# Chunked attention into a token mixer on one core: one more period of stagger between exp and its transposes, and the last batch first in the drain

## The chip, the cores and the metric

One core of a Trainium2 chip runs the whole program. The metric is device time in microseconds. The engines are named as in the profile: PE (TensorE matmuls), PEld (its weight loads), DVE (VectorE), ACT (ScalarE), POOL (GpSimd, which here issues the loads), SP (which issues the stores).

## The reference, cut to what matters

```python
# q, k, v: (8, 8, 576, 64) = batch, heads, tokens, head_dim
# attention inside chunks of 64 tokens: 9 chunks a head
scores = matmul(q_c, k_c.T) / 8
attn   = exp(scores - max(scores)); attn = attn / (sum(attn) + 1e-9)
x      = matmul(attn, v_c)                # then heads side by side: (8, 576, 512)
# token mixer, batch by batch
wq, wk = x @ w_q, x @ w_k                 # (576, 64) each
mixed  = (wq @ wk.T / 8) @ x              # no softmax: the kernel forms wk.T @ x first
out    = relu(mixed) @ w_out              # (8, 576, 512) float32
```

## The kernel before, in words

**Attention.** The 576 chunks (8 batches, 8 heads, 9 chunks) are done 16 at a time in 36 units `u`, 4.5 units to a batch. A unit goes through these stages, each a function of its own:

- `stage_a1`: 16 transposes on PE of q and k into `tp`; `stage_a2`: DVE copies `tp` to `qkt`.
- `stage_b1`: 16 matmuls of 64x64 for the scores into `sp`, DVE takes the row maxima `mx`; `stage_b2`: DVE subtracts them (`sh`), ACT takes exp (`es`).
- `stage_c`: 4 transposes of `es` on PE into `ep`, ACT copies them to `et`.
- `stage_d1`: 16 matmuls with v into `xp` (a column of ones in v gives the row sums); `stage_d2`: three DVE steps (`den`, `rec`, `x_nat`) divide and write the result to the resident `x_nat`.

`tp`, `sp`, `ep` and `xp` have one PSUM buffer each; three more, the tag `m`, serve all steps of the mixer.

**Mixer.** For each batch `make_moe(b)` makes small steps, here called by short names: `xt0`, `xt1`, `xt2` (`p_xt`: six transposes of `x_nat`, one ACT copy of 128x768), `wqk0`, `wqk1` (`p_wqk`: the two projections in two halves; after the second, ACT copies `wqkT` in two pieces and DVE copies `wqd` from it), `wkn` (`p_wkn`: transposes of wk, a DVE copy), `g` (`p_g`: wk.T @ x, an ACT copy), `mix0`, `mix1`, `mixt` (`p_mixed`, `p_mixed_tail`: the mixing matmuls and their relus on ACT), `out0` to `out3` and `outT` (`p_out`, `p_out_tail`: the output projection, an ACT copy `osb`, a store from SP). A full `out` is four matmuls of 512 columns; before, it is cut in two halves.

**Order.** The schedule is manual: every engine runs its instructions in the order in which the Python code emits them. The loop over `kk` makes one period of each unit's stages, and `fill(kk, place, budget)` puts mixer steps between them. The dictionary `plan` gives a step its period and place; the outputs of finished batches wait in `outs` and are taken while a budget lasts. In one period before, PE sees: b1(kk), d1(kk-1), place 0, a1(kk+2), places 1 and 2, c(kk), place 3. DVE sees mx(kk), sh(kk), the three steps of d2(kk-1), the copy of a2(kk+2); ACT sees exp(kk) ahead of the copies of places 1 and 2, then et(kk). After the last period a drain loop emits what is left, in plan order, with outputs between the steps of the chain by estimated costs and due times.

**Loads.** POOL issues the loads of batches 0 to 5 at the start, those of batches 6 and 7 from inside the loop, when the buffers of batches 0 and 1 have been read. The last pieces of batch b are first needed by `stage_a1` of the unit that holds its first chunks, two periods ahead of that unit's b1.

In a cycle of nine periods (two batches) PE's mixer work before is, by the plan, with half outputs written a and b and the position of c marked:

```
16: 2.wkn | 3.xt0 1.out0b c 1.out1a      21: 3.g 4.xt0 2.out1b c 2.out2a
17: 2.g 1.out1b 1.out2a c 1.out2b        22: 3.mix0 | 4.xt1 2.out2b c 2.out3a
18: 2.mix0 | 3.xt1 1.out3a c 1.out3b     23: 3.mix1 | 3.mixt 2.out3b c
19: 2.mix1 | 2.mixt 3.xt2 c 3.wqk0 wqk1  24: 2.outT 4.xt2 3.out0a c 4.wqk0 wqk1
20: 3.wkn | 1.outT 2.out0a 2.out0b c 2.out1a
```

(Left of the bar: place 0, ahead of a1.)

Of the kernel before, what the change touches and what calls it, by code (L numbers as in the profile page):

```python
# [10 lines left out]
F32 = mybir.dt.float32  # L11
AF = mybir.ActivationFunctionType
ALU = mybir.AluOpType
# [4 lines left out]
def kernel(  # L18
# [15 lines left out]
    nc = tc.nc  # L34
# [89 lines left out]
    for b in range(2, 6):  # L124
        loads.append(load(b, None))

    def make_moe(b):
        st = {}

# [18 lines left out]
        def p_wqk(half):  # L148
            def run():
                xt = st["xt"]  # L150
                if half == 0:
                    st["pa"] = m_psum.tile([P, 512], F32, name="wpa", tag="m")
                    st["pb"] = m_psum.tile([P, CH], F32, name="wpb", tag="m")
                pa, pb = st["pa"], st["pb"]
                for i in (2 * half, 2 * half + 1):
                    flags = dict(start=(i == 0), stop=(i == HQ - 1))
                    nc.tensor.matmul(
                        pa[:, :], lhsT=wqk16[:, i, :], rhs=xt[:, NC_ * i : NC_ * i + 8, :], **flags
                    )
                    nc.tensor.matmul(  # L160
                        pb[:, :], lhsT=wqk16[:, i, :], rhs=xt[:, NC_ * i + 8, :], **flags
                    )
                if half == 0:
                    return
                wqkT = moe_pool.tile([P, S], F16, name="wqkT", tag="wqkT")
                wqd = moe_pool.tile([P, S], F16, name="wqd", tag="wqd")
                nc.scalar.copy(wqkT[:, 0:512], pa[:])
                nc.scalar.copy(wqkT[:, 512:S], pb[:])  # L168

                nc.vector.tensor_copy(wqd[CH:P, :], wqkT[0:CH, :])  # L170
                st["wqkT"], st["wqd"] = wqkT, wqd

            return run
# [36 lines left out]
        def p_mixed(w):  # L210
            def run():
                if w == 0:
                    st["rmx"] = moe_pool.tile([P, HQ, S], F16, name="rmx", tag="rmx")
                g16, rmx = st["g16"], st["rmx"]
                wq = (st["wqkT"][0:CH], st["wqd"][CH:P])
                ms = []
                for par in range(2):
                    ma = m_psum.tile([P, 512], F32, name=f"ma{par}", tag="m")
                    nc.tensor.matmul(  # L219
                        ma[:], lhsT=g16[CH * par : CH * par + CH, w, :], rhs=wq[par][:, 0:512]  # L220
                    )
                    ms.append(ma)
                for par in range(2):
                    nc.scalar.activation(  # L224

                        rmx[:, 2 * w + par, 0:512].rearrange("p (c g r) -> p c g r", g=G, r=R),
                        ms[par][:].rearrange("p (c r g) -> p c g r", g=G, r=R),
                        AF.Relu,
                        scale=scale_moe,
                    )  # L230

            return run

        def p_mixed_tail():
            g16, rmx = st["g16"], st["rmx"]
            wq = (st["wqkT"][0:CH], st["wqd"][CH:P])
            for par in range(2):
                mb = m_psum.tile([P, 2, CH], F32, name=f"mb{par}", tag="m")
                for w in range(2):
                    nc.tensor.matmul(  # L240
                        mb[:, w], lhsT=g16[CH * par : CH * par + CH, w, :], rhs=wq[par][:, 512:S]
                    )
                nc.scalar.activation(
                    rmx[:].rearrange("p (w two) s -> p w two s", two=2)[
                        :, :, par, 512:S
                    ].rearrange("p w (g r) -> p w g r", g=G, r=R),
                    mb[:].rearrange("p w (r g) -> p w g r", g=G, r=R),
                    AF.Relu,
                    scale=scale_moe,
                )  # L250

        def p_out(t, half):
            def run():
                rmx = st["rmx"]
                if half == 0:
                    st["op"] = m_psum.tile([P, DM], F32, name="op", tag="m")
                op = st["op"]
                for i in (2 * half, 2 * half + 1):
                    nc.tensor.matmul(  # L259
                        op[:],  # L260
                        lhsT=rmx[:, i, ds(t * P, P)],
                        rhs=wout16[:, i, :],
                        start=(i == 0),
                        stop=(i == HQ - 1),
                    )
                if half == 0:
                    return
                osb = osb_pool.tile([P, DM], F32, name="osb", tag="osb")
                nc.scalar.copy(osb[:], op[:])  # L269
                nc.sync.dma_start(out[b, ds(t * P, P), :], osb[:])  # L270

            return run

        def p_out_tail():
# [21 lines left out]


        chain = [
            (1, 2, 0.4, 0.4, xts[2]),
            (1, 3, 0.5, 0.2, p_wqk(0)),  # L300
            (1, 3, 0.5, 0.6, p_wqk(1)),
            (2, 0, 0.4, 1.2, p_wkn),
            (3, 1, 0.7, 0.9, p_g),
            (4, 0, 0.25, 0.8, p_mixed(0)),
            (5, 0, 0.25, 1.2, p_mixed(1)),
            (5, 1, 0.15, 0.2, p_mixed_tail),
        ]
        outs = [(2, 0.45, p_out(t, half)) for t in range(4) for half in range(2)]
        outs.append((1, 0.5, p_out_tail))
        return xts[:2], chain, outs  # L310

# [73 lines left out]
    def stage_d1(u):  # L385
        et = state[u]["et"]
        xp = x_psum.tile([P, 2, 512], F32, name="xp", tag="xp")
        xv = xp[:, :, 0 : 4 * 65].rearrange("p l (m e) -> p l m e", e=65)
        for m in range(4):
            b, s = divmod(4 * u + m, NS)  # L390
            vt = data[b][1]
            for sl in range(2):
                for par in range(2):
                    rows = slice(CH * par, CH * par + CH)
                    nc.tensor.matmul(  # L395
                        xv[rows, sl, m, :],
                        lhsT=et[rows, m, CH * sl : CH * sl + CH],
                        rhs=vt[rows, sl, s, 0 : D + 1],
                        start=True,
                        stop=True,  # L400
                    )
        state[u]["xv"] = xv
# [17 lines left out]


    moes = [make_moe(b) for b in range(B)]
    ends = [-(-NS * (b + 1) // 4) for b in range(B)]
    plan = {}
    for b in range(B):
        for g in range(2):
            plan.setdefault((-(-(NS * b + 6 * (g + 1)) // 4) + 1, 2), []).append(
                (b, 0.4, 0.0, moes[b][0][g])
            )
        for n, (at, place, cost, wait, step) in enumerate(moes[b][1]):  # L430
            plan.setdefault((ends[b] + at, place), []).append((b, cost, wait, step))
    opened = [0] * B
    outs = []

    def run(entry):
        b, cost, _, step = entry
        step()
        opened[b] += 1
        if opened[b] == 2 + len(moes[b][1]):
            outs.extend(moes[b][2])  # L440
        return cost

    def fill(kk, place, budget):
        spent = sum(run(x) for x in plan.pop((kk, place), []))
        while outs and outs[0][0] == min(place, 2) and spent < budget:
            _, cost, step = outs.pop(0)
            step()
            spent += cost

    for u in range(2):  # L450
        stage_a1(u)
        stage_a2(u)
    for kk in range(NU + 1):
        if kk < NU:
            stage_b1(kk)
        if kk >= 1:
            stage_d1(kk - 1)
        fill(kk, 0, 0.0)
        if kk + 2 < NU:
            stage_a1(kk + 2)  # L460
        if kk < NU:
            stage_b2(kk)
        if kk >= 1:
            stage_d2(kk - 1)
        if kk + 2 < NU:
            stage_a2(kk + 2)
        fill(kk, 1, 0.1)
        fill(kk, 2, 0.8)
        if kk < NU:
            stage_c(kk)  # L470
        fill(kk, 3, 0.4)
        for b in range(B - 6):
            if ends[b] == kk:
                data[b + 6] = load(b + 6, None)

    chain = [x for key in sorted(plan) for x in plan[key]]
    clock, due = 0.0, 0.0
    while chain or outs:
        if chain and (not outs or clock >= due + chain[0][2]):
            entry = chain.pop(0)  # L480
            clock = due = max(clock, due) + run(entry)
        else:
            _, cost, step = outs.pop(0)
            step()
            clock += cost
# [28 lines left out]
```

## Time and profile before

| | |
|---|---|
| median of 3 runs | 187.09 us (185.51 to 187.12) |
| the profiled execution | 186.61 us; span of its instructions 184.8 us |
| busy over the span | PE 79%, DVE 61%, ACT 57%, PEld 50%, POOL 30% |

A row of the timeline has: start in us from the start of the span, duration in us, engine, line, operation, what it writes and reads, how many instructions were merged into the row, and in brackets the idle time of the engine before it with what ended it. PE's matmuls are pipelined, so the distance from one step's start to the next one's start, and not the duration, is what a step takes of PE. The waits list names the waiting instruction, what it waited for, the total in us, how often, and the longest.

### The profile page before, as it was taken

How to read it: one execution, taken by the hardware profiler on the slowest of the kernel's cores; microseconds unless marked ns; L12 is line 12 of the kernel's file. 1: busy time of each engine (PE TensorE's matmuls, PEld its weight loads, DVE VectorE, ACT ScalarE, POOL GpSimd, SP SyncE). 2: the span in 40 equal slices, each digit the busy share in tenths (PEclk: the TensorE clock that was granted, in tenths of full speed). 3: DMA queues.
4: the chain of work that ended last, by engine and by line, in shares of the span. 5: the costliest groups of instructions: out<-in, count | busy, mean ns of one | idle time of the engine just before them, and what ended most of it. 6: DMA issues, size and time to landing. Idle time of an engine off the chain costs nothing. (4 is left out here: it accounts for less than half of the span.)

```text
span 184.8 us, 5746 instructions
## 1 busy us (share of the span) xinstructions
PE 145.2 (79%) x2496; PEld 92.7 (50%) x2496; DVE 112.0 (61%) x233; ACT 105.2 (57%) x209; POOL 55.1 (30%) x68
## 2 busy tenths in 40 slices
PE   0355897896879897969899869798998695988781
PEld 0242675675645555636556546464554463434330
DVE  0123887767984878687868685877686757321000
ACT  2001334454584696647946876479468764584661
POOL 8999999733452603523000000000000000000000
PEclk9999999999999999999999999999999999699999
DMA  3999999999999999999999912032021120232515
GB/s 28 100 123 141 114 144 164 189 181 164 183 163 182 170 233 214 190 190 205 223 210 173 195 59 86 32 122 80 3 89 57 60 88 11 103 131 90 179 71 188
DMA packets 82041, 24.62 MB, mean 133 GB/s; under 512 B 76384, under 2 KB 77920, under 8 KB 82016
## 3 DMA queue, kind: packets, MB, share of 16 engines
q0 software_dynamic: 76128, 14.81, 95.5%
q1 hardware_dynamic: 5888, 9.44, 14.9%
q8 instruction: 19, 0.31, 0.6%
q14 instruction: 6, 0.05, 0.1%
HBM read 29.62 MB, written 9.44 MB: 211 GB/s over the span
## 5 line engine op out<-in xcount | busy, mean ns | idle before, releaser
L373 ACT ACTIVATE es<-sh 128x512 f16<-128x512 f32 x36 | 22.7, 630 | 48.6 <-DVE sh L365 24.3
L327 PE MATMUL tp<-ident,qn 128*64 128x128 f16 x576 | 29.9, 245 | 12.1 <-DMA qn<-in_q_dram 8.4
L259 PE MATMUL op<-wout,rmx 128*128 128x512 f16 x128 | 36.4, 388 | 1.3 <-ACT rmx L224 0.8
L359 DVE TENSOR_REDUCE mx<-sp 128x8 f32<-128x512 f32 x36 | 24.9, 692 | 15.6 <-PE sp L351 15.3
L337 DVE COPY qkt<-tp 128x1024 f16<-128x1024 f16 x36 | 24.5, 682 | 15.7 <-PE tp L327 15.7
L327 PEld LDWEIGHTS <-qn 128*64 128x64 f16 x576 | 21.2, 122 | 18.5 <-DMA qn<-in_q_dram 9.4
L365 DVE TENSOR_TENSOR sh<-sp,mx 128x512 f32<-128x512 f32 x36 | 24.9, 690 | 2.3 <-DVE mx L359 0.5
L410 DVE TENSOR_TENSOR x_nat<-xp,rec 128x512 f16<-128x512 f32 x36 | 24.9, 691 | 1.2
L382 ACT COPY et<-ep 128x512 f16<-128x512 f16 x36 | 21.5, 596 | 6.8 <-PE ep L380 6.4
L380 PE MATMUL ep<-ident,es 128*128 128x128 f16 x144 | 16.0, 241 | 10.0 <-ACT es L373 9.9
L395 PE MATMUL xp<-vt,et 64*64 64x65 f16 x576 | 16.9, 202 | 7.9 <-ACT et L382 7.5
L269 ACT COPY osb<-op 128x512 f32<-128x512 f32 x32 | 19.0, 592 | 5.1 <-PE op L259 2.6
L224 ACT ACTIVATE rmx<-ma 128x512 f16<-128x512 f32 x32 | 17.3, 596 | 8.1 <-PE ma L219 8.1
L380 PEld LDWEIGHTS <-es 128*128 128x128 f16 x144 | 10.4, 107 | 20.5 <-ACT es L373 18.2
L144 ACT COPY xt<-tx 128x768 f16<-128x768 f16 x23 | 18.4, 798 | 2.6 <-PE tx L137 2.5
L395 PEld LDWEIGHTS <-et 64*64 64x64 f16 x576 | 13.0, 115 | 11.4 <-ACT et L382 10.7
L351 PEld LDWEIGHTS <-qkt 64*64 64x64 f16 x576 | 13.0, 116 | 10.4 <-issue 9.2
L351 PE MATMUL sp<-qkt 64*64 64x64 f16 x576 | 17.2, 204 | 0.0
L95 POOL DMA_DIRECT2D vt<-in_v_dram x6 | 11.0, 1835 | 12.7 <-issue 8.0
L259 PEld LDWEIGHTS <-rmx 128*128 128x128 f16 x128 | 10.6, 99 | 7.4 <-issue 2.7
L137 PE MATMUL tx<-ident,x_nat 128*128 128x128 f16 x144 | 13.1, 231 | 1.0 <-ACT rmx L224 0.8
L170 DVE COPY wqd<-wqkT 64x576 f16<-64x576 f16 x8 | 2.8, 354 | 16.3 <-ACT wqkT L168 16.3
(49 smaller groups left out, 163.5 us busy)
## 6 DMA issues: line engine op xcount, KB each, us to landing
out_dram<-osb SPq DMA_DIRECT2D x32, 256.0 KB, 2.2
qn<-in_q_dram POOLq DMA_DIRECT2D x6, 576.0 KB, 18.2
qn<-in_k_dram POOLq DMA_DIRECT2D x6, 576.0 KB, 18.8
vt<-in_v_dram POOLq DMA_DIRECT2D x6, 576.0 KB, 19.5
out_dram<-osbt SPq DMA_DIRECT2D x16, 64.0 KB, 2.1
wout<-in_moe_w_out_dram POOLq DMA_DIRECT2D x2, 256.0 KB, 7.8
qn<-in_q_dram POOLq DMA_DIRECT2D x4, 96.0 KB, 3.2
qn<-in_k_dram POOLq DMA_DIRECT2D x4, 96.0 KB, 3.5
```

The lines of the kernel that those rows point to most:

```text
L259: nc.tensor.matmul(op[:], lhsT=rmx[:, i, ds(t * P, P)], rhs=wout16[:, i, :], start=(i == 0), stop=(i == HQ - 1),)
L269: nc.scalar.copy(osb[:], op[:])
L327: nc.tensor.transpose(tp[CH * sl : CH * sl + CH, j, ti, :, r, :], src[:, sl, t, r * D : r * D + D], ident[:],)
L337: nc.vector.tensor_copy(qkt[:].rearrange("p j t c k -> p (j t c k)"), tp[:].rearrange("p j t c r g -> p (j t c r g)"),)
L351: nc.tensor.matmul(sp[rows, i, :], lhsT=qkt[rows, j, 0, c, :], rhs=qkt[rows, j, 1, c, :], start=True, stop=True,)
L359: nc.vector.tensor_reduce(mx[:], sp[:], axis=AX.X, op=ALU.max)
L365: nc.vector.tensor_tensor(out=sh[:].rearrange("p i (g r) -> p i r g", g=G, r=R), in0=sp[:].rearrange("p i (r g) -> p i r g", g=G, r=R), in ...
L373: nc.scalar.activation(es[:], sh[:], AF.Exp, scale=scale_attn)
L380: nc.tensor.transpose(ep[:, m, :], es[:, 2 * m : 2 * m + 2, :], ident[:])
L382: nc.scalar.copy(et[:], ep[:])
L395: nc.tensor.matmul(xv[rows, sl, m, :], lhsT=et[rows, m, CH * sl : CH * sl + CH], rhs=vt[rows, sl, s, 0 : D + 1], start=True, stop=True,)
L410: nc.vector.tensor_tensor(out=x_nat[:, 4 * u : 4 * u + 4, :, :].rearrange("p m l d -> p l m d"), in0=xv[:, :, :, 0:D], in1=rec[:, :, :, No ...
```

## The change

Unit kk's transposes of exp, `stage_c`, move from the end of period kk to the middle of period kk+1, ahead of `stage_b2`; `stage_d1` and `stage_d2` follow one period later, and the loop has one period more. The places inside a period are ordered anew, the outputs are no longer halved and are taken only if they fit the budget, and the plan's dates are recomputed by `period`. In the last batch (`b == B - 1`) half of the relus, the small `wqkT` copy and every second `osb` copy go to DVE. The drain now runs the last batch's steps as soon as their due time comes, with everything else as filling.

```diff
+    def relu(on_vector, to, of):
+        if on_vector:
+            nc.vector.tensor_scalar(to, of, scale_moe, 0.0, op0=ALU.mult, op1=ALU.max)
+        else:
+            nc.scalar.activation(to, of, AF.Relu, scale=scale_moe)
...
-                nc.scalar.copy(wqkT[:, 512:S], pb[:])
+                (nc.vector.tensor_copy if b == B - 1 else nc.scalar.copy)(wqkT[:, 512:S], pb[:])
...
-                    nc.scalar.activation(
+                    relu(
+                        b == B - 1 and par == 1,
...
-        def p_out(t, half):
+        def p_out(t):
...
-                for i in (2 * half, 2 * half + 1):
+                for i in range(HQ):
...
-                nc.scalar.copy(osb[:], op[:])
+                (nc.vector.tensor_copy if b == B - 1 and t % 2 else nc.scalar.copy)(osb[:], op[:])
...
         chain = [
-            (1, 2, 0.4, 0.4, xts[2]),
-            (1, 3, 0.5, 0.2, p_wqk(0)),
-            (1, 3, 0.5, 0.6, p_wqk(1)),
+            (1, 2, 0.4, 0.2, xts[2]),
+            (1, 2, 0.5, 0.4, p_wqk(0)),
+            (1, 2, 0.5, 0.0, p_wqk(1)),
             (2, 0, 0.4, 1.2, p_wkn),
             (3, 1, 0.7, 0.9, p_g),
             (4, 0, 0.25, 0.8, p_mixed(0)),
-            (5, 0, 0.25, 1.2, p_mixed(1)),
-            (5, 1, 0.15, 0.2, p_mixed_tail),
+            (5, 0, 0.25, 0.8, p_mixed(1)),
+            (5, 1, 0.15, 0.5, p_mixed_tail),
         ]
-        outs = [(2, 0.45, p_out(t, half)) for t in range(4) for half in range(2)]
+        outs = [(2, 0.9, p_out(t)) for t in range(4)]
...
-    ends = [-(-NS * (b + 1) // 4) for b in range(B)]
+        period = lambda slots: -(-slots // 4) + 1
...
-        while outs and outs[0][0] == min(place, 2) and spent < budget:
+        while outs and outs[0][0] == place and spent + outs[0][1] <= budget:
...
-    for kk in range(NU + 1):
+    for kk in range(NU + 2):
         if kk < NU:
             stage_b1(kk)
-        if kk >= 1:
-            stage_d1(kk - 1)
+        if kk >= 2:
+            stage_d1(kk - 2)
         fill(kk, 0, 0.0)
         if kk + 2 < NU:
             stage_a1(kk + 2)
+        fill(kk, 1, 0.7)
+        if 1 <= kk <= NU:
+            stage_c(kk - 1)
         if kk < NU:
             stage_b2(kk)
-        if kk >= 1:
-            stage_d2(kk - 1)
+        if kk >= 2:
+            stage_d2(kk - 2)
         if kk + 2 < NU:
             stage_a2(kk + 2)
-        fill(kk, 1, 0.1)
-        fill(kk, 2, 0.8)
-        if kk < NU:
-            stage_c(kk)
-        fill(kk, 3, 0.4)
+        fill(kk, 2, 1.4 if len(outs) < 4 else 1.9)
...
-    chain = [x for key in sorted(plan) for x in plan[key]]
+    rest = [x for key in sorted(plan) for x in plan[key]]
+    last = [x for x in rest if x[0] == B - 1]
+    rest = [x for x in rest if x[0] < B - 1]
     clock, due = 0.0, 0.0
-    while chain or outs:
-        if chain and (not outs or clock >= due + chain[0][2]):
-            entry = chain.pop(0)
+    while last or rest or outs:
+        if last and (clock >= due + last[0][2] or not (rest or outs)):
+            entry = last.pop(0)
             clock = due = max(clock, due) + run(entry)
+        elif rest:
+            clock += run(rest.pop(0))
```

By the new plan PE's mixer work in nine periods is as follows; the first bar stands for a1, and c(kk-1) stands where it is written:

```
16: | c 2.xt2 2.wqk0 2.wqk1              21: 3.wkn | c 2.out0 2.out1
17: 2.wkn | c 3.xt0 1.out2               22: | 3.g c 4.xt0 2.out2
18: | 2.g c 1.out3                       23: 3.mix0 | c 4.xt1 2.out3
19: 2.mix0 | 1.outT c 3.xt1              24: 3.mix1 | 3.mixt 2.outT c 3.out0 3.out1
20: 2.mix1 | 2.mixt c 3.xt2 3.wqk0 wqk1
```

In the last periods and the drain it is:

```
35: b1 d1(33) 6.wkn c(34) 7.xt0 5.out2
36: d1(34) 6.g c(35) 5.out3
37: d1(35) 6.mix0 5.outT 7.xt1
drain: 6.mix1 7.xt2 6.mixt 6.out0 7.wqk0 7.wqk1 6.out1 6.out2 7.wkn 6.out3 7.g 6.outT
       7.mix0 7.mix1 7.mixt 7.out0 7.out1 7.out2 7.out3 7.outT
```

More of the change, by code (lines that the diff above doesn't have):

```diff
@@ L223, in run @@
                 for par in range(2):
-                    nc.scalar.activation(
+                    relu(
+                        b == B - 1 and par == 1,
                         rmx[:, 2 * w + par, 0:512].rearrange("p (c g r) -> p c g r", g=G, r=R),
                         ms[par][:].rearrange("p (c r g) -> p c g r", g=G, r=R),
-                        AF.Relu,
-                        scale=scale_moe,
                     )
@@ L242, in p_mixed_tail @@
                     )
-                nc.scalar.activation(
+                relu(
+                    b == B - 1 and par == 1,
                     rmx[:].rearrange("p (w two) s -> p w two s", two=2)[
@@ L247, in p_mixed_tail @@
                     mb[:].rearrange("p w (r g) -> p w g r", g=G, r=R),
-                    AF.Relu,
-                    scale=scale_moe,
                 )
-        def p_out(t, half):
+        def p_out(t):
             def run():
                 rmx = st["rmx"]
-                if half == 0:
-                    st["op"] = m_psum.tile([P, DM], F32, name="op", tag="m")
-                op = st["op"]
-                for i in (2 * half, 2 * half + 1):
+                op = m_psum.tile([P, DM], F32, name="op", tag="m")
+                for i in range(HQ):
                     nc.tensor.matmul(
@@ L265, in run @@
                     )
-                if half == 0:
-                    return
                 osb = osb_pool.tile([P, DM], F32, name="osb", tag="osb")
-                nc.scalar.copy(osb[:], op[:])
+                (nc.vector.tensor_copy if b == B - 1 and t % 2 else nc.scalar.copy)(osb[:], op[:])
                 nc.sync.dma_start(out[b, ds(t * P, P), :], osb[:])
@@ L422 @@
     moes = [make_moe(b) for b in range(B)]
-    ends = [-(-NS * (b + 1) // 4) for b in range(B)]
     plan = {}
     for b in range(B):
+        period = lambda slots: -(-slots // 4) + 1
         for g in range(2):
-            plan.setdefault((-(-(NS * b + 6 * (g + 1)) // 4) + 1, 2), []).append(
+            plan.setdefault((period(NS * b + 6 * (g + 1)) + 1, 2), []).append(
                 (b, 0.4, 0.0, moes[b][0][g])
             )
-        for n, (at, place, cost, wait, step) in enumerate(moes[b][1]):
-            plan.setdefault((ends[b] + at, place), []).append((b, cost, wait, step))
+        for at, place, cost, wait, step in moes[b][1]:
+            plan.setdefault((period(NS * (b + 1)) + at, place), []).append((b, cost, wait, step))
     opened = [0] * B
@@ L460 @@
             stage_a1(kk + 2)
+        fill(kk, 1, 0.7)
+        if 1 <= kk <= NU:
+            stage_c(kk - 1)
         if kk < NU:
             stage_b2(kk)
-        if kk >= 1:
-            stage_d2(kk - 1)
+        if kk >= 2:
+            stage_d2(kk - 2)
         if kk + 2 < NU:
             stage_a2(kk + 2)
-        fill(kk, 1, 0.1)
-        fill(kk, 2, 0.8)
-        if kk < NU:
-            stage_c(kk)
-        fill(kk, 3, 0.4)
+        fill(kk, 2, 1.4 if len(outs) < 4 else 1.9)
         for b in range(B - 6):
-            if ends[b] == kk:
+            if 4 * (kk - 1) >= NS * (b + 1) > 4 * (kk - 2):
                 data[b + 6] = load(b + 6, None)
-    chain = [x for key in sorted(plan) for x in plan[key]]
+    rest = [x for key in sorted(plan) for x in plan[key]]
+    last = [x for x in rest if x[0] == B - 1]
+    rest = [x for x in rest if x[0] < B - 1]
     clock, due = 0.0, 0.0
-    while chain or outs:
-        if chain and (not outs or clock >= due + chain[0][2]):
-            entry = chain.pop(0)
+    while last or rest or outs:
+        if last and (clock >= due + last[0][2] or not (rest or outs)):
+            entry = last.pop(0)
             clock = due = max(clock, due) + run(entry)
+        elif rest:
+            clock += run(rest.pop(0))
         else:
```

## The prediction

> **What bounds the kernel now.** I read the page's totals first, then the waits, then one cycle of nine periods in the windows view and in PE's timeline.
>
> ```profile
> PE 145.2 (79%) x2496; PEld 92.7 (50%) x2496; DVE 112.0 (61%) x233; ACT 105.2 (57%) x209; POOL 55.1 (30%) x68
> ```
> ```profile
> 76.75:114.19 37.44, 32.40 (x627) 20.72 (x625) 28.09 (x58) 25.59 (x52) 4.22 (x3) 1.00 1.48 171
> ```
> ```profile
> PEld L380 <- ACT es L373: 18.2, 25, 1.9
> DVE wqd L170 <- ACT wqkT L168: 16.3, 8, 3.4
> PEld L395 <- ACT et L382: 10.7, 21, 0.8
> ```
>
> The second row is the cycle from b1(16) to b1(25): 37.44 us, of which PE is busy 32.40, DVE 28.09, ACT 25.59. PE is nearest to full, but idle for 5 us, and the waits say on what: stage c's weight loads wait for exp (18.2 us in the run), stage d1's for et (10.7). Both come from doing exp, c, et and d1 within little more than a period. The middle row is another kind: DVE stops in front of `wqd` until ACT has copied `wqkT`, about 2 us in each batch, and the next period's mx stands behind it. What PE needs without waits is read from starts in its timeline:
>
> ```profile
> 76.75 0.44 PE L351 MATMUL sp<-qkt 64*64 64x64 f16 x16
> ...
> 77.46 0.40 PE L184 MATMUL wknp<-ident,wqkT 64*128 64x64 f16 x8
> ...
> 77.94 0.64 PE L327 MATMUL tp<-ident,qn 128*64 128x128 f16 x16
> ...
> 80.73 0.40 PE L380 MATMUL ep<-ident,es 128*128 128x128 f16 x4 [1.28 <-ACT es L373]
> ...
> 83.23 0.60 PE L199 MATMUL gp<-x_nat,wkn 128*64 128x256 f16 x8
> ...
> 83.99 1.04 PE L259 MATMUL op<-wout,rmx 128*128 128x512 f16 x4
> 84.86 0.39 PE L380 MATMUL ep<-ident,es 128*128 128x128 f16 x4
> 85.09 0.59 PE L259 MATMUL op<-wout,rmx 128*128 128x512 f16 x2
> 85.61 0.44 PE L351 MATMUL sp<-qkt 64*64 64x64 f16 x16
> 85.98 0.44 PE L395 MATMUL xp<-vt,et 64*64 64x65 f16 x16
> 86.35 0.39 PE L219 MATMUL ma<-wqkT,g 64*128 64x512 f16 x1
> ...
> 86.67 0.64 PE L327 MATMUL tp<-ident,qn 128*64 128x128 f16 x16
> 87.24 0.51 PE L137 MATMUL tx<-ident,x_nat 128*128 128x128 f16 x6
> 87.59 0.59 PE L259 MATMUL op<-wout,rmx 128*128 128x512 f16 x2
> ...
> 95.33 0.60 PE L281 MATMUL opt<-wout,rmx 128*64 128x256 f16 x8
> 95.86 1.04 PE L259 MATMUL op<-wout,rmx 128*128 128x512 f16 x4
> ...
> 112.94 0.38 PE L157 MATMUL wpa<-xt,wqk 128*128 128x512 f16 x1
> ...
> 114.19 0.44 PE L351 MATMUL sp<-qkt 64*64 64x64 f16 x16
> ```
>
> From each start to the next: b1 0.37, d1 0.37, mix 0.32, a1 0.57, xt 0.35, wkn 0.48, g 0.76, out 0.87, c 0.23, outT 0.53, both halves of wqk 1.25. `mixt` has no undisturbed row; I put it at 0.40, between c's 0.23 and wkn's 0.48. The row at 80.73 shows the wait to be removed: 1.28 us in front of c(16).
>
> **The steady part after the change.** In the new order c(kk-1) needs the exp of the period before, and d1 the et of the period before. Exp stands ahead of the copies of place 2 on ACT, so both are ready when PE comes: I cost these two waits at nothing, covered by a whole period of PE work. PE's base is b1 + d1 + a1 + c = 1.54; with the plan's steps the nine periods 16 to 24 sum to
>
> 16: 3.14, 17: 3.24, 18: 3.17, 19: 2.74, 20: 3.86, 21: 3.76, 22: 3.52, 23: 3.08, 24: 4.53; together 31.0.
>
> That is a floor. Two other things are late next.
>
> ```profile
> 46.10 0.69 DVE L359 TENSOR_REDUCE mx<-sp 128x8 f32<-128x512 f32 x1
> ...
> 49.11 0.69 DVE L359 TENSOR_REDUCE mx<-sp 128x8 f32<-128x512 f32 x1
> ```
> ```profile
> L189 DVE COPY wkn<-wknp 128x576 f16<-128x576 f16 x2 | 0.9, 448 | 0.0
> ```
> ```profile
> 115.00 0.30 DVE L170 COPY wqd<-wqkT 64x576 f16<-64x576 f16 x1 [1.84 <-ACT wqkT L168]
> ...
> 115.33 0.69 DVE L359 TENSOR_REDUCE mx<-sp 128x8 f32<-128x512 f32 x1
> ```
>
> DVE, back to back, takes 3.01 us from one mx to the next (46.10 to 49.11), and 3.45 with wkn's copy. And `wqd` stays where it was, at the end of its period: wqk ended at 114.19, the next mx began 1.14 us later, at 115.33. Ahead of that the second half of wqk now waits for xt2's copy, which on ACT stands behind et and exp:
>
> ```profile
> L373 ACT ACTIVATE es<-sh 128x512 f16<-128x512 f32 x36 | 22.7, 630 | 48.6 <-DVE sh L365 24.3
> L382 ACT COPY et<-ep 128x512 f16<-128x512 f16 x36 | 21.5, 596 | 6.8 <-PE ep L380 6.4
> L269 ACT COPY osb<-op 128x512 f32<-128x512 f32 x32 | 19.0, 592 | 5.1 <-PE op L259 2.6
> L224 ACT ACTIVATE rmx<-ma 128x512 f16<-128x512 f32 x32 | 17.3, 596 | 8.1 <-PE ma L219 8.1
> L144 ACT COPY xt<-tx 128x768 f16<-128x768 f16 x23 | 18.4, 798 | 2.6 <-PE tx L137 2.5
> ```
>
> Period 16, from b1: sh ends at about 1.9 (b1's 0.44, then mx and sh at 0.7 each), exp at 2.55, xt2's copy at 3.35, the second half of wqk at 4.0, the next mx 1.14 later; less the half microsecond by which an undisturbed mx trails its b1, 4.65 from mx to mx. In period 20 ACT also has two relus of `mix1` and the small ones of `mixt` ahead of et: the copy ends near 4.4 and PE near 5.0, but DVE comes out of periods 17 to 19 already late, so I take 5.1 from mx to mx, bounded by 4.65 and by 5.7, the sum without that lateness. The periods then become, each the larger of PE's and DVE's: 4.65, 3.45, 3.17, 3.01, 5.1, 3.76, 3.52, 3.08, 4.53, sum 34.3. Changing from out to b1 costs PE some 0.09 more (85.09 to 85.61 is 0.52 for two matmuls where four took 0.87), five times: 34.7 against 37.44.
>
> From period 8 (mx at 46.10) to b1(35) at 155.75, whose mx comes half a microsecond later, there are three such nines, the first with fewer outputs: 110.1 us now, 3 x 34.7 = 104.1 after. **Steady part: -6.0 us.** Ends: -7.3 without the 0.09s, about 0 if the waits come back elsewhere.
>
> **The start gains nothing.** Up to period 7 loads set the pace:
>
> ```profile
> 30.28 1.35 POOL L91 DMA_DIRECT2D qn<-in_k_dram  x1
> ```
> ```profile
> DMA to landing us min/median/max: 10.4/18.8/20.7
> ```
>
> Batch 2's k, issued at 30.28, lands at 40.7 at the earliest, and stage a1 of period 7 needs it. In the new order c(6), xt2 and wqk stand behind that a1 on PE, where before all of these came first; what the early periods save is lost there. I take 0, between -1 and +1.5. The loads of batches 6 and 7 are emitted a period later, but POOL, still at batch 2 at 30.28, gets to them long after those periods; stores keep their number on SP.
>
> **The drain.**
>
> ```profile
> 155.75 0.44 PE L351 MATMUL sp<-qkt 64*64 64x64 f16 x16
> ...
> 158.25 1.89 PE L259 MATMUL op<-wout,rmx 128*128 128x512 f16 x4
> ...
> 174.09 0.39 PE L219 MATMUL ma<-wqkT,g 64*128 64x512 f16 x1 [0.47 <-ACT g L207]
> ...
> 176.63 3.61 PE L259 MATMUL op<-wout,rmx 128*128 128x512 f16 x16 [0.27 <-ACT rmx L224]
> ```
> ```profile
> 157.70:161.10 3.40, 3.37 (x16) 1.29 (x12) 0.92 (x3) 2.02 (x4) 0.00 (x0) 0.57 0.09 36
> ```
>
> From b1(35) to the last batch's outputs: 20.88 us. Four out matmuls at 158.25 took 1.89 where they took 1.04 at 83.99, because the granted clock was 0.57 from 157.70 to 161.10, after a stage c that waited for exp. With that wait gone I expect no such dip, worth about 1.3 us by these rows. After: period 35 is 2.67, period 36 2.23, period 37 1.57, the drain to `outT` of batch 6 7.57, together 14.04. From mix0 to the outputs took 2.54; with half of the relus on DVE at 0.69 (as mx, which reads the same shape from PSUM) beside ACT's 0.60 I take 2.0. That makes 16.0, a gain of 4.8. The added period is inside this sum: its c, d1 and d2 are hidden by batch 5's and 6's outputs, and without that cover would cost 3 to 3.6. ACT is crowded around batch 6's relus (two pairs, xt1, half of xt2, `mixt`, one output), which I charge with 1.3. **Drain: -3.5 us**, ends -4.8 and 0.
>
> Sum: 186.61 - 6.0 - 3.5 = 177.1, against the profiled execution, 0.5 below the median of 187.09. **I forecast 177 us**, a case of 173.5 to 180.5.
>
> [...]
>
> **The rivals.**
>
> *The waits come back halfway.* PE's three `m` buffers are freed by ACT, whose copies now stand behind et and exp. If that costs 0.15 us a period over 27 periods, the steady part keeps 2; with a drain of -1 to -2, 183. For it: ACT has 25.59 of 37.44 us, and 48.6 us of idle time stand in front of exp, behind which everything else on ACT must queue. Against: in period 21 exp ends about 3.6 us after b1 (mx at 1.14, wkn's copy 0.45, mx and sh 0.7 each, exp 0.63), the copy of `out0` at 4.2, and its buffer is next needed by xt0 of period 22, at about 6.1 (3.76 + 1.54 + 0.76). Chance 0.17.
>
> *Slower: ACT's order becomes the wait.* Its place is the first mixer matmul after a1, waiting for a buffer whose copy stands behind exp. It decides where the exp of a period with outputs ends more than 5 us after b1, that is where DVE trails b1 by over 2.5 us (I have 1.14 after wqk). At 0.3 us a period it takes 8 us, all of the steady gain and 2 more, and PE then comes late to the drain, whose added period finds no cover (3 to 3.6) and whose clock dips again: 189.5, 188 to 192. Chance 0.07.
>
> *It does not do what it says:* exp itself is so late that c still waits a period later, or wqk's wait grows by what c's shrinks. Then the nine stays at 37.4, and the drain gives what the added period takes: 187. Chance 0.06.
>
> *Better:* half of what DVE and wqk add to PE's floor (34.3 - 31.0) is absorbed, 1.6 a nine: 172. Chance 0.05. The forecast keeps 0.65.
>
> **How the numbers follow.** The range runs from 172, the better case, to 184, the upper side of the halfway case, and leaves out under 2 in 10. About 1% is what a measurement of this kernel can tell from no change (185.2 to 189). Faster: 0.65 + 0.05 + 0.15 of the halfway case = 0.85; same: 0.05 of the fourth case, 0.02 of the halfway and 0.01 of the slow one = 0.08; slower 0.07.
>
> **What would show it.** Right: from b1(16) to b1(25) about 34.7 us; c's wait for exp under 4 us in all and d1's for et under 2; DVE's wait in front of `wqd` still about 16; wqk's second half with a new wait of about 1 us for xt2's copy; no clock dip near the end; 17 to 18 us from b1(35) to the last batch's outputs. Wrong: a nine of 36 or more, with waits of PE's mixer matmuls for ACT's copies; a dip of the clock around period 7; an end later than 22 us after b1(35).

## The result: 179.1 us against 187.1, and the profile after

The changed kernel took 179.10 us (median of 4 runs, 178.93 to 179.23), the kernel before 187.11 (185.51 to 188.18): a ratio of 0.958, 95% interval 0.951 to 0.965. The forecast was 177.0 with a range of 172 to 184. The profiled execution took 179.23 us, its span is 177.5. A ratio here counts undisturbed executions alone, and as most of the kernel before's beside experiments 1 to 4 and one of experiment 8's (381.95 us) were disturbed, it need not be the ratio of two medians.

The page of the changed kernel, PE's busy tenths and its granted clock in 40 slices (the clock shows 9 from the start, although PE's own rows, shown under "The start" below, are longer until about 34 us: b1 took 0.63 us at 32.53 and 0.44 at 34.91):

```profile
PE   0364987953977799997997999799979996798990
PEclk9999999995699999999999999999999999999999
```

The windows view of the changed kernel; columns are the length, then busy time of PE, PEld, DVE, ACT and POOL with their counts, PE's clock, DMA share and GB/s:

```profile
77.60:111.89 34.29, 31.23 (x625) 20.89 (x624) 27.39 (x58) 25.74 (x53) 3.22 (x3) 1.00 1.55 189
150.13:169.12 18.99, 16.34 (x197) 9.06 (x195) 7.46 (x19) 13.49 (x28) 0.00 (x0) 1.00 0.26 94
40.70:47.50 6.80, 3.87 (x30) 2.47 (x30) 1.71 (x5) 1.80 (x3) 3.11 (x4) 0.50 2.19 168
```

The first row is b1(16) to b1(25): 34.29 us where it was 37.44. PE's idle time in it fell from 5.0 to 3.1 us, and its busy time from 32.4 to 31.2. The second is b1(35) to the last batch's outputs, the third a stretch at a granted clock of 0.50, for which the same view of the kernel before has 1.00; its wqk matmuls took 0.38 us from 41.13 us on.

Its list of waits:

```profile
DVE wqd L176 <- ACT wqkT L174: 14.3, 7, 3.6
PE wpa L163 <- ACT xt L150: 7.2, 7, 1.5
PE xp L395 <- DVE x_nat L410: 3.5, 6, 1.2
PEld L395 <- ACT et L382: 1.7, 5, 0.5
PEld L395 <- ACT es L373: 4.6, 5, 1.6
```

Stage c's wait for exp (18.2 us before) has no row left among the larger ones, d1's for et fell from 10.7 to 1.7, `wqd`'s is nearly as it was, and wqk waits for xt2's copy, 7 times, 7.2 us. The last row is new: d1's weight loads also wait 4.6 us in 5 places that are put down to exp, 1.6 of it between b1(8) and b1(35).

Divided at the same instructions, the two traces differ by stage as follows (us; the end is from the last batch's outputs to the end of the span):

| | before | after | difference | forecast |
|---|---|---|---|---|
| start, to b1(8) | 45.62 | 47.64 | +2.0 | 0 (-1 to +1.5) |
| b1(8) to b1(35) | 110.13 | 102.49 | -7.6 | -6.0 (-7.3 to 0) |
| b1(35) to the last outputs | 20.88 | 18.99 | -1.9 | -3.5 (-4.8 to 0) |
| the end | 8.21 | 8.34 | +0.1 | 0 |

So the sum was off by 2 us, the start by 2.0 and the drain by 1.6 the wrong way, the steady part by 1.6 the right way. The start (+2.0) and the steady part (-7.6) both fell outside the ends given for them; their errors offset each other.

### The profile page after: what moved, and what is told of

The parts are those of the page before. It is cut to its first block, busy times and chain, and to the rows that moved or that the text cites. A ratio compares the mean times of both kernels' runs of the same rounds, so it can differ in the third digit from the quotient of the medians.

```text
span 177.5 us, 5756 instructions
## 1 busy us (share of the span) xinstructions
PE 140.1 (79%) x2496; PEld 92.2 (52%) x2496; DVE 113.8 (64%) x239; ACT 102.9 (58%) x203; POOL 55.2 (31%) x68
## 4 chain that ended last, share of the span: by engine, by line
PE 32%; ACT 28%; POOL 17%; DVE 10%; DMA 7%; issue 3%; ACTq 0%; POOLq 0%; DVEq 0%
PE op L261 11%; ACT rmx L131 9%; POOL qn L103 8%; DMA qn<-in_k_dram 7%; ACT xt L150 6%; ACT es L373 5%; POOL vt L105 5%; PE tp L327 4%; PE wpa L163 3%; PE xp L395 2%; ACT et L382 2%; PE ep L380 2%; DVE mx L359 2%; PE sp L351 2%; DVE sh L365 2%
## 5 line engine op out<-in xcount | busy, mean ns | idle before, releaser
L327 PE MATMUL tp<-ident,qn 128*64 128x128 f16 x576 | 30.8, 242 | 17.1 <-DMA qn<-in_q_dram 9.0
L327 PEld LDWEIGHTS <-qn 128*64 128x64 f16 x576 | 21.7, 120 | 25.5 <-DMA qn<-in_q_dram 10.4
L261 PE MATMUL op<-wout,rmx 128*128 128x512 f16 x128 | 31.2, 379 | 0.3 <-ACT xt L148 0.2
L269 ACT COPY osb<-op 128x512 f32<-128x512 f32 x30 | 17.4, 586 | 5.2 <-PE op L261 4.0
L395 PE MATMUL xp<-vt,et 64*64 64x65 f16 x576 | 16.2, 198 | 5.2 <-DVE x_nat L410 3.5
L131 ACT ACTIVATE rmx<-ma 128x512 f16<-128x512 f32 x30 | 16.5, 610 | 1.2 <-PE ma L225 1.1
L261 PEld LDWEIGHTS <-rmx 128*128 128x128 f16 x128 | 11.6, 98 | 10.4 <-issue 0.2
L163 PE MATMUL wpa<-xt,wqk 128*128 128x512 f16 x32 | 10.8, 407 | 7.2 <-ACT xt L150 7.2
L380 PE MATMUL ep<-ident,es 128*128 128x128 f16 x144 | 15.3, 234 | 0.0
L143 PE MATMUL tx<-ident,x_nat 128*128 128x128 f16 x144 | 12.6, 227 | 0.4 <-ACT xt L150 0.3
```

Of the source, the lines that this page charges most:

```text
L131: nc.scalar.activation(to, of, AF.Relu, scale=scale_moe)
L261: nc.tensor.matmul(op[:], lhsT=rmx[:, i, ds(t * P, P)], rhs=wout16[:, i, :], start=(i == 0), stop=(i == HQ - 1),)
L327: nc.tensor.transpose(tp[CH * sl : CH * sl + CH, j, ti, :, r, :], src[:, sl, t, r * D : r * D + D], ident[:],)
L395: nc.tensor.matmul(xv[rows, sl, m, :], lhsT=et[rows, m, CH * sl : CH * sl + CH], rhs=vt[rows, sl, s, 0 : D + 1], start=True, stop=True,)
```

## The experiments

My theory: the stagger takes away the waits in the steady part; the start lost because PE's order puts three steps behind a load; wqk's second half now waits for ACT; the drain lost its expected gain to DVE. The rivals: the drain or the unhalved outputs made the gain; the load itself was late; DVE's stop at `wqd` is what sets the pace.

**1 and 2. The two halves of the change.**

```diff
# stagger alone: the changed kernel with
-    while last or rest or outs: ...            # the new drain
+    while chain or outs: ...                   # the drain of before
-                        b == B - 1 and par == 1,
+                        False,                 # and all relus and copies on ACT
# drain alone: the kernel before with the new drain and the last batch shared with DVE
```

> The changed kernel with the drain loop of before and with the last batch's relus and copies all on ACT: the stagger and its plan alone. If the gain is the stagger's (steady part -7.6 us in the traces, start +2.0), this gives 180 to 181.5 us, and nine periods still take 34.3 us. If the drain and its two engines carried the gain, it is back at 184 or more.

> The kernel before, with only the new drain loop and the last batch's work shared with DVE. If the gain is the stagger's: 186 to 187 us, nine periods unchanged at 37.4, and the clock dip near the end stays, since stage c of unit 34 still waits for exp. If the drain's order was worth the 1.7 us that the end gained: 185 to 185.5. If it was the main thing: 182.

The stagger alone took 180.93 us, ratio 0.978 (0.966 to 0.990); its trace has b1(8) at 48.19 and 102.42 us to b1(35), as the whole change has. It came 1.8 us behind the whole change, and so keeps between 4 and 6 of its 8 us: 4.1 by its ratio, 6.2 by the two medians.

The drain alone took 185.53 us in the median (184.32 to 187.09), ratio 1.001 (0.994 to 1.008): no difference in the time is shown. Its trace departs from the expectation. Nine periods took 39.04 us, with a granted clock of 0.6 in two slices of its page in them (83.4 to 88.0 and 97.3 to 101.9 us), and no slice near the end is under 0.9, although c(34) waited for exp as it did in the kernel before (1.44 us at 154.99 there):

```profile
157.90 0.40 PE L383 MATMUL ep<-ident,es 128*128 128x128 f16 x4 [1.44 <-ACT es L376]
```

From b1(35) to the last outputs it took 18.32 us; the kernel before, with the dip, took 20.88. The steady part belongs to the stagger with its plan.

**3. The start.**

```diff
-        if kk + 2 < NU:
+        if kk + 2 < NU and kk != 7:
             stage_a1(kk + 2)
...
         fill(kk, 2, 1.4 if len(outs) < 4 else 1.9)
+        if kk == 7:
+            stage_a1(kk + 2)
+            stage_a2(kk + 2)
```

> The changed kernel with stage a1 and a2 of period 7 emitted after that period's mixer steps, so that c(6), xt2 and both halves of wqk no longer stand on PE behind the wait for batch 2's k. If that order cost the start its 2.0 us (and halved the clock), b1(8) moves from 47.6 to 44 or 45 us, the dip after 40 us goes, and the time is 176 to 177. If the load itself came too late and everything after it needs it, it stays at 179 (178.5 to 179.5).

It took 175.63 us, ratio 0.948 (0.932 to 0.964). PE's timeline of the changed kernel around the load, and then that of this experiment:

```profile
38.91 0.44 PE L395 MATMUL xp<-vt,et 64*64 64x65 f16 x16 [0.69 <-DVE x_nat L410]
40.05 0.30 PE L327 MATMUL tp<-ident,qn 128*64 128x128 f16 x4 [0.70 <-DMA qn<-in_q_dram]
43.28 0.85 PE L327 MATMUL tp<-ident,qn 128*64 128x128 f16 x12 [2.93 <-DMA qn<-in_k_dram]
44.06 0.61 PE L380 MATMUL ep<-ident,es 128*128 128x128 f16 x4
...
47.64 0.44 PE L351 MATMUL sp<-qkt 64*64 64x64 f16 x16
```
```profile
41.81 0.38 PE L163 MATMUL wpa<-xt,wqk 128*128 128x512 f16 x1 [1.65 <-ACT xt L150]
...
42.39 0.30 PE L327 MATMUL tp<-ident,qn 128*64 128x128 f16 x4
43.55 0.85 PE L327 MATMUL tp<-ident,qn 128*64 128x128 f16 x12 [0.86 <-DMA qn<-in_k_dram]
44.34 0.63 PE L351 MATMUL sp<-qkt 64*64 64x64 f16 x16
```

The load ended the wait at about the same time in both, 43.28 and 43.55. In the changed kernel c(6), xt2 and wqk came after it and took 3.58 us (44.06 to 47.64); in the experiment they were done, and b1(8) came 3.3 us earlier, nearly all of the 3.5 gained; the time is a little under the expected 176 to 177. The order, not the load, cost the start. The dip of the clock was not removed: the page of this experiment has a granted clock of 0.5 and 0.7 in the slices from 43.6 to 52.3 us, a little later, and 0.7 and 0.8 in those from 30.5 to 39.2.

**4. The copy of xt2.**

```diff
-            (1, 2, 0.4, 0.2, xts[2]),
+            (1, 1, 0.4, 0.2, xts[2]),
```

> The changed kernel with the step xt2 of every batch moved from place 2 to place 1, ahead of stage c, so that on ACT its copy stands ahead of et and exp. If the wait of wqk's second half (1.0 to 1.5 us in each of seven periods) is on the path, it falls under 0.3 and the time is 174 to 176.5, with nine periods near 33. If DVE's stop in front of wqd only takes it over, the wait goes and the time stays within 1 us of 179.

It took 174.32 us, ratio 0.942 (0.929 to 0.955), inside what the first theory expected. First PE and ACT in period 16 of the changed kernel, then the same period here:

```profile
79.82 0.19 PE L166 MATMUL wpb<-xt,wqk 128*128 128x64 f16 x1
81.14 0.38 PE L163 MATMUL wpa<-xt,wqk 128*128 128x512 f16 x1 [1.12 <-ACT xt L150]
```
```profile
79.28 0.59 ACT L382 COPY et<-ep 128x512 f16<-128x512 f16 x1 [0.94 <-PE ep L380]
79.77 0.63 ACT L373 ACTIVATE es<-sh 128x512 f16<-128x512 f32 x1
80.30 0.79 ACT L150 COPY xt<-tx 128x768 f16<-128x768 f16 x1
```
```profile
79.09 0.38 PE L163 MATMUL wpa<-xt,wqk 128*128 128x512 f16 x1 [0.17 <-ACT xt L150]
```
```profile
78.24 0.80 ACT L150 COPY xt<-tx 128x768 f16<-128x768 f16 x1 [1.00 <-PE tx L143]
78.94 0.59 ACT L382 COPY et<-ep 128x512 f16<-128x512 f16 x1
79.41 0.64 ACT L373 ACTIVATE es<-sh 128x512 f16<-128x512 f32 x1
```

The copy now goes ahead of et and exp, and wqk's wait falls from 1.12 to 0.17. From b1(8) to b1(35) it takes 97.92 us against 102.49. What et and exp lose does not show: d1's wait for et is 1.8 us in all, against 1.7. The stagger gives each a whole period.

**5. DVE's stop at wqd.**

```diff
-                nc.vector.tensor_copy(wqd[CH:P, :], wqkT[0:CH, :])
...
             nc.vector.tensor_copy(wkn[:], wp[:])
+            nc.vector.tensor_copy(st["wqd"][CH:P, :], st["wqkT"][0:CH, :])
```

> The changed kernel with DVE's copy wqd emitted after wkn's copy in the next period, so that no mx stands behind ACT's wqkT. If PE's list and the wait for xt2's copy set the pace of the periods after wqk, DVE's stop (14.3 us in all) goes but the time falls by 1 to 2 us only, to 177 to 178.5, most of it from the 1.15 us that d1(34) waits. If DVE's stop still sets the pace, as the forecast's chains had it, 0.66 us a batch and more goes: 174 or less.

It took 179.29 us, ratio 0.957 (0.950 to 0.964): no gain over 179.10, and both theories missed. Its nine periods from b1(17), and two of its waits:

```profile
81.26:115.60 34.34, 31.26 (x628) 20.93 (x626) 27.77 (x58) 25.68 (x52) 3.01 (x2) 1.00 1.40 180
```
```profile
DVE mx L359 <- PE sp L351: 20.7, 19, 3.3
PE wpa L163 <- ACT xt L150: 7.2, 7, 1.5
```

DVE's wait for `wqkT` has left its list (it now waits for PE's scores instead), the nine periods take what they took (34.29 in the changed kernel, from b1(17) as from b1(16)), and PE's wait for xt2's copy is the same 7.2 us. A large row of DVE's waits was slack.

**6 and 9. The two parts of the drain.** Experiment 6 keeps the new order with everything on ACT, experiment 9 the old order with the second engine; the edits are those of experiment 1, one at a time.

> The changed kernel with its new drain order, but with all relus and copies of the last batch on ACT. The two engines are worth 0.5 us by the relu rows and about 0.3 by the wqkT copy: 179.7 to 180.2. If the second engine and not the order makes the 1.8 us between the change and its version with the old drain: 181.

> The changed kernel with the drain loop of before, but the last batch still shared between ACT and DVE: the missing fourth of the two parts of the drain. If the parts add, with 182.45 for the new order alone and 180.93 for neither, this is 177.5 to 178. If the new order pays only together with the second engine, it is 179.5 to 180.5, between neither and both.

| | all on ACT | shared with DVE |
|---|---|---|
| drain loop of before | 180.93 (180.73 to 181.63) | 180.89 (179.77 to 181.76) |
| new drain loop | 182.45 (181.23 to 183.90) | 179.10 (178.93 to 179.23) |

The ratios to the kernel before are 0.978 (0.966 to 0.990), 0.965 (0.958 to 0.973), 0.976 (0.963 to 0.988) and 0.958. Experiment 6 came 2.3 us above its first expectation and 1.5 above its second, experiment 9 0.4 above the upper end of its second. In these medians only both parts together gain. The trace of experiment 6 says why it came out slow, at least in that run: its last outputs ran at a granted clock of 0.69.

```profile
170.14:175.27 5.13, 5.13 (x17) 1.85 (x17) 0.00 (x0) 2.05 (x5) 0.00 (x0) 0.69 0.17 63
```

The same sixteen matmuls took 3.54 us in the changed kernel (169.12 to 172.66), at a granted clock of 1.00. Without those 1.6 us its profiled 181.75 would be 180.2, at the upper end of what was expected. From the last batch's mix0 to its outputs experiments 1 and 6 took 2.54 us, the changed kernel 1.85 and experiment 9 1.86: the second engine's 0.7 us there is plain. The traces of experiments 1 and 9 have a dip in their drain too (a granted clock of 0.50 from 151.8 to 155.2 us in experiment 1, a mean of 0.89 from 150 to 181 in experiment 9), and the changed kernel has none (1.00 from 150.13 to 177.25). Over its four executions the mean granted clock is 0.979 to 0.989 in the changed kernel, 0.971 to 0.990 in experiment 1, 0.947 to 0.978 in experiment 9 and 0.925 to 0.972 in experiment 6. So the table mixes the two parts with the clock, and whether the second engine keeps the clock up stays open.

**7 and 8. The repairs together.** Experiment 8 has edits 3 and 4, experiment 7 edits 3, 4 and 5.

> The changed kernel with both repairs: a1 of period 7 after that period's mixer steps, and xt2 at place 1. If the two waits are independent, their gains of 3.5 and 4.8 us add: 170.5 to 171.5. If they share the same time (the wait for xt2's copy in period 7 counts in both), 172 to 173.

> Both repairs and wqd after wkn's copy. If DVE's stop is off the path once xt2 is early, no more than 0.5 us below the version with two repairs. If it is the next bound, 1.5 to 3 us below it.

Experiment 8 took 170.50 us, ratio 0.909 (0.901 to 0.917): the gains of 3.5 and 4.8 add. Its trace has b1(8) at 43.66 and 97.49 us from there to b1(35), and a granted clock of 0.9 or more in every slice of its page. Experiment 7 took 171.88 (170.56 to 173.47), ratio 0.915 (0.903 to 0.927), 1.4 more than experiment 8 where up to 0.5 less was expected. Its trace has nine periods of 32.91 us for 32.84: taking `wqd` away gains nothing there either. Why two of its four executions took 173 is not shown.

**10. The change without its stagger.**

```diff
-        period = lambda slots: -(-slots // 4) + 1
+        period = lambda slots: -(-slots // 4)
-        if 1 <= kk <= NU:
-            stage_c(kk - 1)
...
         fill(kk, 2, 1.4 if len(outs) < 4 else 1.9)
+        if kk < NU:
+            stage_c(kk)
# stage_d1 and stage_d2 of kk - 1 in period kk; NU + 1 periods
```

> The changed kernel without the stagger: c(kk) stands at the end of period kk, behind all mixer steps, d1 and d2 follow in the next period, and the plan's dates move back by one; unhalved outputs, places, budgets, new drain and two engines stay. If the stagger removes the waits, they come back here: d1 waits about 0.5 us for et in each period, nine periods take 37 to 38 us and the time is 185 to 189. If the new places and the unhalved outputs carry the gain, nine periods stay under 35.5 and the time under 182.

It took 196.08 us, ratio 1.048 (1.040 to 1.056): slower than either kernel, beyond both theories. Its waits, one of them in PE's timeline, and nine of its periods:

```profile
PEld L395 <- ACT et L382: 24.6, 36, 1.0
```
```profile
109.17 0.44 PE L395 MATMUL xp<-vt,et 64*64 64x65 f16 x16 [0.77 <-ACT et L382]
```
```profile
85.91:126.25 40.34, 32.43 (x627) 21.58 (x626) 27.83 (x59) 25.70 (x53) 1.81 (x1) 1.00 1.02 128
```

Every one of the 36 units waits for et in front of d1. The kernel before put half outputs behind c to cover this; the new places have nothing there. So the unhalved outputs and new places do not carry the gain: on their own they lose, and they are affordable only with the stagger. The stagger with the old places and halved outputs was not run, so what each is worth apart stays open.

**11. One more repair.** With g of batch 6 ahead of d1(34) in period 36:

```diff
+        if kk == NU:
+            fill(kk, 1, 0.7)
         if kk >= 2:
             stage_d1(kk - 2)
```

> The version with the two repairs (170.5 us) and, in period 36, the step g of batch 6 ahead of d1(34), which waits 1.15 us there for xp. If that wait is on the path, g (0.79 us) fills it: 169.3 to 170. If the last batch's chain ends no earlier because DVE sets x_nat(35), it stays at 170.5.

It took 169.53 us (169.29 to 169.69), ratio 0.905 (0.900 to 0.910), the best of all. Its PE in period 36:

```profile
143.73 0.63 PE L205 MATMUL gp<-x_nat,wkn 128*64 128x256 f16 x8
...
144.88 0.44 PE L395 MATMUL xp<-vt,et 64*64 64x65 f16 x16 [0.30 <-DVE x_nat L410]
```

g stands where d1 had waited, 1.18 us in experiment 8's trace; 0.30 is left, and b1(35) to the last outputs falls from 19.19 to 18.50. It does not overlap with experiment 8, whose other three executions took 169.96 to 170.55; the 1 us between the medians is a little more than the 0.7 that the traces show here.

## Why the prediction was right, and where it was not

**The steady part** held in its mechanism: nearly all of c's and d1's waits went. It gained 7.6 us, 1.6 more than forecast. That nine periods came so near their sum, 34.29 us for 34.7, is partly luck, as the parts were less right. PE's list with its five changes from out to b1 makes 31.5; the waits for xt2's copy in periods 16 and 20 add 2.2, and smaller waits the rest. The chain up to wqk was right: its end was put at 4.0 after b1 in period 16 and near 5.0 in period 20, and from b1 to b1 they took 4.12 and 5.28.

The step that failed is DVE's: "`wqd` stays where it was" was costed as part of the pace, as 1.14 us more up to the next mx less the half microsecond by which mx trails b1, and so was DVE's floor of 3.01. Period 19 took 2.62 from b1 to b1 (b1 runs ahead and DVE's lateness is made up later), and experiment 5 shows that the stop at `wqd` costs nothing. Waits that were not in the sum took the place of these terms, as in period 18, put at 3.17, which took 3.62 because d1 waited for `x_nat`. The wait for xt2's copy, named in the same chain, is the one that counts (experiment 4), 4.6 us over the steady part.

**The start** failed: "I take 0, between -1 and +1.5" was +2.0. The mechanism stood in the text, that c(6), xt2 and wqk queue behind a1's wait; its size was not worked out. The load landed 12.9 us after its issue (30.36 to 43.28). With some 0.4 us for the rest of a1 and the 2.92 that c, xt2 and wqk took in period 16 at a clock of 1.00 (78.80 to 81.72, of which 1.12 is the wait for xt2's copy), b1(8) could not come before about 46.6. The rest is the clock, granted at 0.50 from 40.7 to 47.5, which the prediction had among its signs of being wrong: the same steps took 3.58 us, and the rest of a1 0.78, about 1.0 more together.

That is against this kernel at a clock of 1.00, and not against the kernel before, whose PE was slow until 41.1 us: wqk's matmul of 512 columns took 0.61 us there at 40.65, as long as the 0.59 to 0.63 of the changed kernel at a granted clock of 0.50, and 0.38 at 41.13. PE's timeline of the kernel before, then b1 of periods 5 and 6 in the changed kernel:

```profile
40.65 0.61 PE L157 MATMUL wpa<-xt,wqk 128*128 128x512 f16 x1
...
41.13 0.38 PE L157 MATMUL wpa<-xt,wqk 128*128 128x512 f16 x1
...
42.91 0.64 PE L327 MATMUL tp<-ident,qn 128*64 128x128 f16 x16
```
```profile
32.53 0.63 PE L351 MATMUL sp<-qkt 64*64 64x64 f16 x16
...
34.91 0.44 PE L351 MATMUL sp<-qkt 64*64 64x64 f16 x16
```

The changed kernel left the slow rows at about 34 us (b1 0.63 us, then 0.44) and had the clock of 0.50 for 6.8, so up to b1(8) the two were slow for about as long (41.1 us against 34 and 6.8), and the clock alone does not explain the 2.0. In the kernel before c, xt2 and wqk were done when a1 of period 7 ran, at 42.91, without a wait for its load.

**The drain** was mis-sized: -1.9 for -3.5. PE's timeline of the changed kernel:

```profile
151.90 1.03 PE L261 MATMUL op<-wout,rmx 128*128 128x512 f16 x4
154.11 0.44 PE L395 MATMUL xp<-vt,et 64*64 64x65 f16 x16 [1.19 <-DVE x_nat L410]
...
159.35 0.49 PE L143 MATMUL tx<-ident,x_nat 128*128 128x128 f16 x6 [0.33 <-ACT xt L150]
...
160.35 0.22 PE L245 MATMUL mb<-wqd,g 64*128 64x64 f16 x2 [0.27 <-ACT rmx L131]
160.81 1.02 PE L261 MATMUL op<-wout,rmx 128*128 128x512 f16 x4 [0.25 <-ACT xt L148]
...
167.27 0.39 PE L225 MATMUL ma<-wqkT,g 64*128 64x512 f16 x1
...
169.12 3.61 PE L261 MATMUL op<-wout,rmx 128*128 128x512 f16 x16
```

From b1(35) at 150.13 to the last batch's mix0 at 167.27 it took 17.14 us for a list of 14.04. The charge of 1.3 for ACT's crowd was about right: the three small waits around 160 and the spread of the steps between them come to some 1.7. The term that was too small is period 35: put at 2.67, it took 3.98 (150.13 to 154.11), for the 1.19 us in front of d1(34). d1(34) needs `xp`, which `x_nat` of unit 33 frees, and on DVE that stands behind mx(35), wkn's copy and sh(35); the step g, which could fill the time, was placed behind d1(34) (experiment 11). The stop at `wqd` is not the reason: experiment 5, without that stop, has the same wait.

```profile
153.77 0.44 PE L395 MATMUL xp<-vt,et 64*64 64x65 f16 x16 [1.21 <-DVE x_nat L410]
```

The last 2.0 us, from mix0 to the outputs with relus on two engines, came out at 1.85.

The clock dip of before was gone, as forecast, but not for the reason given. The prediction tied it to c's wait for exp; experiments 1, 6 and 9 have the stagger and a dip in their drain (0.50, 0.69 and 0.89 in the stretches given with experiments 6 and 9), and experiment 2 has the wait, 1.44 us, and none. That the changed kernel's trace has none is luck as far as these traces show.

**The rivals.** The halfway case (183) and the slow one (189.5) did not come: the waits of PE's mixer matmuls for a buffer are a few tenths each. That the change would not do what it says is refuted by the waits: c's for exp is gone and d1's for et is 1.7. The better case (172) did not come; it supposed that half of what DVE and wqk add to PE's list is absorbed, and it took a further edit, xt2's copy moved ahead, to bring nine periods to 32.8 (experiments 4, 8 and 11). Of the signs of being wrong one came, the dip of the clock around period 7, and the stretch from b1(35), called right at 17 to 18 us, took 18.99.

**The relus** cost about what the prediction put down for them, 0.69 and 0.60: DVE's of 128x512 from float32 in PSUM took 0.69 us, ACT's 0.61.

## What to carry to other kernels

When an extra stage of stagger is added, look at what an in-order queue now puts behind a load and behind a long wait: here moving one transposing stage past three others in one single period was worth 3.5 us, and moving one copy ahead of two that had gained a period of slack 4.8. A large row in the list of waits need not be on the path; take it out once before building on it. List PE's work from start to start, as it gives the floor of a period, and check the periods without filling, at both ends, one by one. Where the clock matters, read it from the durations of like rows too: in the kernel before the windows view has 1.00 from 32.00 to 41.13 us, where wqk's matmul took 0.61 us (at 40.65), and 1.00 also behind that, where it took 0.38.

## What the runs showed of the hardware

The granted clock was 0.57 from 157.70 to 161.10 us in the kernel before, 0.50 from 40.70 to 47.50 in the changed one, 0.50 from 151.8 to 155.2 in experiment 1 and 0.69 from 170.14 to 175.27 in experiment 6. Ahead of these dips PE was only partly idle. A stretch of about 3.4 us just ahead of one, in the kernel before, the changed one and experiment 6, and last a stretch of the changed kernel that no dip followed:

```profile
153.80:157.20 3.40, 1.75 (x42) 1.18 (x44) 2.31 (x6) 2.29 (x4) 0.00 (x0) 1.00 0.06 24
```
```profile
37.28:40.70 3.42, 1.25 (x38) 0.82 (x36) 3.25 (x8) 1.12 (x2) 0.34 (x1) 1.00 1.82 185
```
```profile
166.60:170.00 3.40, 2.57 (x24) 1.06 (x21) 0.00 (x0) 3.06 (x8) 0.00 (x0) 0.99 0.46 160
```
```profile
147.00:150.40 3.40, 1.88 (x34) 1.19 (x33) 2.01 (x5) 2.10 (x4) 0.00 (x0) 1.00 0.44 157
```

PE was busy for 1.25 to 2.57 us of the 3.4 ahead of these dips, and for 1.88 where none came. So its busy time in such a stretch does not tell these rows apart, and what brings a dip is not shown.
